# Linear attention into a routed expert layer on one core: the first route's exponential is issued after the search for the fullest expert, and the experts' first rows are read from PSUM

## The chip, the core and the metric

The kernel runs on one core of a Trainium2 chip. The metric is the device time of one execution in microseconds (us); lower is better. Names of engines in the profile: PE is TensorE (PEld its weight loads), DVE is VectorE, ACT is ScalarE, POOL is GpSimd, SP is the engine that issues most of the DMAs. SBUF is the on-chip memory that every engine reads; PSUM is the small one that TensorE writes its products to, and that DVE and ACT can read and write.

## The reference

Four batches of 576 tokens with 8 heads of 64 go through attention with a feature map, and the 2304 rows of 512 that come out are routed, each to one of 8 experts (a two-layer network with 1024 hidden units). An expert takes at most `capacity` = 576 rows, in the order of the tokens.

```
phi(x):  proj = x @ w_phi;  proj -= max(abs(proj));  [exp(proj), exp(-proj)]
kv = phi(k)^T v;  z = sum phi(k);  x = (phi(q) kv) / (phi(q) z + 1e-6)

logits = x @ w_gate;  expert = argmax(logits)
gate   = exp(0) / (sum exp(logits - max) + 1e-9)
row    = number of earlier tokens with the same expert   (kept if < capacity)
disp[expert, row] = x
out[token] = gate * relu(disp[expert] @ w1[expert]) @ w2[expert]
```

## The kernel before

**Two stages.** In the first (about 4 to 168 us) attention runs and every token is routed: its row is scattered into a buffer `xs` in device memory, where each expert has 576 slots. In the second (168 us to the end) the experts run one after the other over their rows, and their results are scattered to the output.

**The pipeline of the first stage.** The tokens are cut into two passes `p` of 9 blocks of 128 tokens. A pass has 18 items for the keys and then 18 for the queries, one per block and half of the heads. In each step `t` of `attention()` a new item begins on TensorE with `project` (L259 and L260: products with the two halves of `w_phi`, into a PSUM tile `pr` of which there are two). One step later DVE centres it (`center`: the maximum `m`, L265, then the difference `d`, L269; there are three tiles for `d`). ACT makes the two exponentials `kp` of a key item (L315, L316), or, after a transpose on TensorE (L356), `qp` of a query item (L358, L359). Four steps after its projection TensorE sums a key item (`kv_sum`, L342); a query item is multiplied with the sums by `q_num` (L371). Beside this ACT and POOL split the next inputs into two 16-bit parts: L194 on ACT writes the high part, and L195 on POOL, which waits for it, the low one.

**Routing in small steps.** `rows_out` leaves the logits of a block in `lg`, and `route` is called for groups of 9, 4, 3 and 2 blocks. It does no work itself: it appends some 25 small operations to the list `pending`, and `tick()`, which is called after each operation of `center` and within `rows_out`, takes the next ones from it. So the list's order and its length decide between which large instructions a small one stands on its engine. From step 36 on, `tick()` is sparing: it takes one operation at every second call (two in steps 46 and 49) until the first group knows the fullest expert, and one per call after that. An entry `rest` does nothing but spend a turn.

**The first group and the fullest expert.** The experts are run with the fullest of the first 9 blocks first. For that the first group alone has the five operations of `swaps()`: a product of ones with the counts `rb` on TensorE, into the columns `TOT` of the PSUM tile `sm` (L502), the maximum (L503), its place (L504, L505), and nine small POOL instructions (`swap_all`, L488 to L496). These leave in SBUF the expert order and, in `perm["s"]`, the first row of each expert in `xs`. Each route later multiplies its one-hot choice `oh` (16-bit, SBUF) with `perm["s"]` (L539) and sums it (L540): the first row of the token's expert. The product on TensorE that numbers the tokens (`positions`, L455) writes the same tile `sm` as L540.

**The shared tile.** The small operands of all routes lie in one PSUM tile, `sm_t` (named `sm`): logits less their maximum (`lt`), choice, counts, sums, and the columns `TOT`. The framework orders accesses by tile. `exps` (L481) is the exponential of `lt` on ACT: it reads `sm` and writes `es`, which `sums` (L470) needs only after `positions`.

Of the kernel before, what the change touches and what calls it, by code (L numbers as in the profile page):

```python
# [15 lines left out]
ALU = mybir.AluOpType  # L16
# [4 lines left out]
P = 128  # L21
# [3 lines left out]
NE, DM, DFF = 8, H * D, 1024  # L25
# [12 lines left out]
def tile_kernel(ctx: ExitStack, tc: tile.TileContext, qT, kT, vT, vv, w_phi, w_g, w1, w2, out, cap):  # L38
# [55 lines left out]
    perm = {x: cpool.tile([P, NE], F32, tag=f"perm{x}", name=f"perm{x}") for x in "abcdesh"}  # L94
# [46 lines left out]
    POS, SCR, SW, TOT = 0, 72, 210, 496  # L141
    sm_t = ps_1.tile([P, 512], F32, tag="sm", name="sm")
# [240 lines left out]
    def rows_out(p, r):  # L383
# [14 lines left out]
        if i == n - 1:  # L398
            route(blk - i, n, xr, lg)
# [15 lines left out]
    def route(blk, n, xr, lg):  # L415
        def small(name, shape, dt=F32):
            return r_p.tile([P, n, *shape], dt, tag=name, name=name)
# [15 lines left out]
        oh = small("oh", [NE], BF16)  # L433
        rb = r_p.tile([P, NE], BF16, tag="rb", name="rb")
        es, sel = small("es", [NE]), small("sel", [NE])
# [4 lines left out]
        v = nc.vector  # L440

        def flat(t):
            return t.rearrange("p n a -> p (n a)")
# [55 lines left out]
        def swaps():  # L499
            tot = sm_t[:, TOT:TOT + NE]  # L500
            return [
                lambda: nc.tensor.matmul(tot, ones, rb, start=True, stop=True),  # L502
                lambda: v.tensor_reduce(seen, tot, AX.X, ALU.max),  # L503
                lambda: v.scalar_tensor_tensor(perm["a"], tot, seen, iota8, ALU.is_ge, ALU.mult),  # L504
                lambda: v.tensor_reduce(lead8, perm["a"], AX.X, ALU.min),  # L505
                swap_all,
            ]

        late = blk >= LATE
# [12 lines left out]
        def ready():  # L522
# [9 lines left out]
            lambda: v.scalar_tensor_tensor(ef, lt, 0.0, io, ALU.is_ge, ALU.mult),  # L532
            lambda: v.tensor_reduce(flat(ix), ef, AX.X, ALU.min),
            lambda: v.tensor_tensor(oh, ix.to_broadcast([P, n, NE]), io, ALU.is_equal),
            *([number, exps] if late else [exps] if old is None else []),
            lambda: v.tensor_reduce(rn[:, 0], oh.rearrange("p n e -> p e n"), AX.X, ALU.add),
            run_total,
            *([*swaps(), rest, rest, rest] if old is None else []),
            lambda: v.tensor_tensor(sel, oh, perm["s"].unsqueeze(1).to_broadcast([P, n, NE]), ALU.mult),  # L539
            lambda: v.tensor_reduce(flat(sl), sel, AX.X, ALU.add),  # L540
            positions,
            *([] if late or old is None else [exps, rest, rest, rest]),
# [571 lines left out]
```

## Time and profile before

| | |
|---|---|
| median of 3 runs | 427.6 us (426.96 to 427.92) |
| the profiled execution's own time | 425.98 us |
| its span, first to last instruction | 424.2 us |
| mean granted TensorE clock | 0.99 of full |
| PE busy | 405.1 us (95%) |
| DVE busy | 265.9 us (63%) |
| ACT busy | 245.9 us (58%) |
| POOL busy | 175.4 us (41%) |

The profile is of one execution, and its own time is 1.6 us below the median. Starts and durations are in us from the span's first instruction. A duration on DVE or ACT contains a fixed part in which the next instruction already runs, so the distance between two starts is the better measure of what an instruction takes from its engine. Time in which an engine stood still before an instruction is shown in brackets with what ended it; an instruction that had begun and was held up inside shows a long duration instead. `PEclk` is the clock that TensorE was granted, as a share of 2.4 GHz: 0.50 is the lower of its two levels, 1.2 GHz.

### The profile page before, as it was taken

What the parts mean: (1) busy time and instruction counts of PE and PEld (TensorE: products, weight loads), DVE (VectorE), ACT (ScalarE), POOL (GpSimd) and SP (SyncE); (2) the same over time, 40 slices, a digit from 0 to 9 for tenths busy, and PEclk for the clock granted to TensorE, in tenths of its full rate; (3) what the DMA queues carried; (4) which work ended last, traced back from release to release, by engine and by line L of the source; (5) the groups of instructions that cost most, each with busy time, mean ns of one, the idle gap of its engine ahead of it and who ended that gap; (6) DMA issues with size and microseconds to landing.
All of it is one profiled execution on the core that took longest, in us unless ns stands there. A gap on an engine that the chain in (4) does not pass through costs nothing.

```text
span 424.2 us, 12166 instructions
## 1 busy us (share of the span) xinstructions
PE 405.1 (95%) x4813; PEld 357.7 (84%) x4813; DVE 265.9 (63%) x585; ACT 245.9 (58%) x452; POOL 175.4 (41%) x215
## 2 busy tenths in 40 slices
PE   6999999999799989999999999999999999999992
PEld 4788888888789878989979898989898998799871
DVE  5776898887788797833247975757475464156410
ACT  3978687779776766712146855656565454155410
POOL 1848566448576778730035306042241500160011
PEclk9999999999899999999999999999999999999997
DMA  7990599489506743479007995977959176210010
GB/s 254 388 353 5 170 328 372 138 287 307 172 6 222 227 171 107 175 249 368 5 32 223 341 338 192 331 226 224 324 179 349 64 240 228 93 36 0 2 51 29
DMA packets 42715, 82.78 MB, mean 195 GB/s; under 512 B 4351, under 2 KB 9343, under 8 KB 42624
## 3 DMA queue, kind: packets, MB, share of 16 engines
q1 hardware_dynamic: 38080, 72.13, 50.5%
q0 software_dynamic: 4544, 9.47, 6.2%
q8 instruction: 53, 0.87, 0.9%
q14 instruction: 38, 0.31, 0.2%
HBM read 62.65 MB, written 24.30 MB: 205 GB/s over the span
## 4 chain that ended last, share of the span: by engine, by line
PE 83%; POOL 4%; issue 4%; ACT 4%; DVE 3%; DMA 1%; POOLq 0%; ACTq 0%
PE ph L814 9%; PE ph L815 9%; PE ph L817 9%; PE acc L342 8%; PE acc L371 5%; PE sm L847 4%; PE sm L845 4%; PE sm L848 4%; PE ph L845 4%; PE ph L847 4%; PE ph L848 4%; PE pr L259 3%; PE pr L260 2%; PE pr L254 2%; PE pt L747 2%
## 5 line engine op out<-in xcount | busy, mean ns | idle before, releaser
L169 POOL DMA_INDIRECT out<-y,it x22 | 24.4, 1111 | 164.4 <-ACT y L860 86.7
L123 DVE TENSOR_TENSOR l<-raw,h 128x512 fp32r<-128x512 f32 x118 | 79.6, 706 | 19.6 <-ACT h L117 16.9
L195 POOL TENSOR_TENSOR stk<-px,stk 64x1024 f16<-64x1024 f32 (+1 forms) x30 | 70.8, 2363 | 38.6 <-ACT stk L194 37.7
L814 PE MATMUL ph<-xh,h 128*128 128x256 f32 (+3 forms) x292 | 79.4, 298 | 0.1
L815 PE MATMUL ph<-xh,l 128*128 128x256 f32 (+3 forms) x292 | 78.9, 296 | 0.0
L117 ACT ACTIVATE h<-raw 128x512 fp32r<-128x512 f32 x128 | 75.7, 629 | 0.0
L828 ACT ACTIVATE h<-ph 128x256 fp32r<-128x256 f32 (+3 forms) x67 | 28.8, 429 | 53.6 <-PE ph L817 52.9
L831 DVE SCALAR_TENSOR_TENSOR h<-ph,h 128x256 fp32r<-128x256 f32 (+2 forms) x91 | 33.3, 388 | 39.2 <-ACT h L828 38.8
L814 PEld LDWEIGHTS ph<-xh,h 128*128 128x128 f32 x292 | 55.6, 191 | 1.2 <-issue 0.2
L815 PEld LDWEIGHTS ph<-xh,l 128*128 128x128 f32 x292 | 55.7, 191 | 0.9
L265 DVE TENSOR_REDUCE m<-pr 128x4 f32<-128x512 f32 x72 | 49.2, 684 | 8.6 <-PE pr L260 5.1
L269 DVE TENSOR_TENSOR d<-pr,m 128x512 f32<-128x512 f32 x72 | 49.7, 691 | 4.0 <-ACT kp L316 0.4
L817 PE MATMUL ph<-xh,h 128*128 128x256 f32 (+3 forms) x292 | 50.9, 296 | 0.0
L342 PE MATMUL acc<-v,kp 128*64 128x73 f32 (+1 forms) x1280 | 46.3, 231 | 1.1 <-issue 1.1
L342 PEld LDWEIGHTS acc<-v,kp 128*64 128x64 f32 (+1 forms) x1280 | 40.7, 138 | 5.8 <-issue 2.6
L371 PE MATMUL acc<-kv,qp 128*64 128x73 f32 x1152 | 44.5, 229 | 0.0
L371 PEld LDWEIGHTS acc<-kv,qp 128*64 128x64 f32 x1152 | 39.1, 136 | 6.0 <-issue 5.7
L817 PEld LDWEIGHTS ph<-xh,h 128*128 128x128 f32 x292 | 42.7, 191 | 0.6
L259 PE MATMUL pr<-whi,stk 128*128 128x128 f16 x260 | 36.9, 223 | 2.6 <-DVE d L269 2.3
L260 PE MATMUL pr<-wlo,stk 128*128 128x128 f16 x260 | 36.4, 221 | 0.0
L194 ACT ACTIVATE stk<-px 64x1024 f16<-64x1024 f32 (+1 forms) x30 | 34.5, 1150 | 0.5
L358 ACT ACTIVATE qp<-pt 128x512 f32<-128x512 f32 x36 | 21.5, 596 | 21.1 <-PE pt L356 21.0
(163 smaller groups left out, 715.8 us busy)
## 6 DMA issues: line engine op xcount, KB each, us to landing
raw<-in_w SPq DMA_DIRECT2D x28, 1024.0 KB, 7.9
xs<-fill SPq DMA_DIRECT2D x18, 514.0 KB, 6.1
xr<-xs SPq DMA_DIRECT2D x24, 257.0 KB, 7.9
raw<-in_w SPq DMA_DIRECT2D x8, 512.0 KB, 4.3
vt<-in_vT SPq DMA_DIRECT2D x3, 1152.0 KB, 12.7
v<-in_vv SPq DMA_DIRECT2D x2, 1314.0 KB, 11.9
px<-in_kT SPq DMA_DIRECT2D x5, 512.0 KB, 8.5
px<-in_qT SPq DMA_DIRECT2D x4, 640.0 KB, 9.3
```

Source lines behind the costliest of these rows:

```text
L117: nc.scalar.activation(hi, a, AF.Copy)
L123: engine.tensor_tensor(lo, a, hi.bitcast(F32), ALU.subtract)
L195: return lambda: nc.gpsimd.tensor_tensor(t[other], x, t[own], ALU.subtract)
L259: nc.tensor.matmul(pr[:, j], lt, whi, start=True, stop=False)
L260: nc.tensor.matmul(pr[:, j], lt, wlo, start=False, stop=True)
L265: nc.vector.tensor_reduce(m.rearrange("p a b -> p (a b)"), pr, AX.X, ALU.max, apply_absolute_value=True)
L269: beat[0] = nc.vector.tensor_tensor(d, pr, m.to_broadcast([P, 4, NF]), ALU.subtract)
L342: nc.tensor.matmul(acc[f:f + D, a, j * GC:(j + 1) * GC], kp[lo:hi, j, a, f:f + D], vt[lo:hi, r, h * GC:(h + 1) * GC], start=first and j == ...
L371: nc.tensor.matmul(num[lo:hi, g, j * GC:(j + 1) * GC], qp[:, a, j, lo:hi], kv_t[b][:, a, 4 * g + j], start=(a == 0), stop=(a == 1))
L814: nc.tensor.matmul(acc, hi[:, k, fs], xh[:, k, o:o2], start=(k == 0), stop=False)
L815: nc.tensor.matmul(acc, lo[:, k, fs], xh[:, k, o:o2], start=False, stop=False)
L817: nc.tensor.matmul(acc, hi[:, k, fs], xl[:, k, o:o2], start=False, stop=(k == 3))
```

## The change

Three things change in the list of `route`. In the first group `exps` moves from its place ahead of the count (L536) to behind `swap_all`. Behind the three `rest`s a new operation copies `perm["s"]` from SBUF into the columns `TOT` of the PSUM tile `sm`, which by then have been read by L503 and L504. And in all four groups the product `sel` reads the first rows from there, not from `perm["s"]`.

```
-            *([number, exps] if late else [exps] if old is None else []),
+            *([number, exps] if late else []),
             lambda: v.tensor_reduce(rn[:, 0], oh.rearrange("p n e -> p e n"), AX.X, ALU.add),
             run_total,
-            *([*swaps(), rest, rest, rest] if old is None else []),
-            lambda: v.tensor_tensor(sel, oh, perm["s"].unsqueeze(1).to_broadcast([P, n, NE]), ALU.mult),
+            *([*swaps(), exps, rest, rest, rest, lambda: v.tensor_copy(sm_t[:, TOT:TOT + NE], perm["s"])]
+              if old is None else []),
+            lambda: v.tensor_tensor(sel, oh, sm_t[:, TOT:TOT + NE].unsqueeze(1).to_broadcast([P, n, NE]), ALU.mult),
```

In the changed kernel the copy is L538 and `sel` L540; the lines behind them have a number one higher than before. `old is None` holds for the first group, `late` for the last.

The first place is on DVE in the second pass's keys, from the first group's choice `oh` (L534) to its count `rb` (L476); `m` and `d` are the large operations of `center`, and in brackets stands which engine's semaphore a row waits for. Before:

```order
L534 TENSOR_TENSOR oh<-sm,iota_74 128x72 [waits DVE_49]
L269 TENSOR_TENSOR d<-pr,m 128x512 [waits DVE_49,Activation_49]
L265 TENSOR_REDUCE m<-pr 128x4 [waits PE_49]
L536 TENSOR_REDUCE sm<-oh 128x8 [waits DVE_49,Activation_49]
L269 TENSOR_TENSOR d<-pr,m 128x512 [waits DVE_49]
L265 TENSOR_REDUCE m<-pr 128x4 [waits PE_49]
L476 CAST rb<-sm 128x8 [waits DVE_49]
```

On the same engine at the same place, with the change:

```order
L534 TENSOR_TENSOR oh<-sm,iota_74 128x72 [waits DVE_49]
L269 TENSOR_TENSOR d<-pr,m 128x512 [waits DVE_49,Activation_49]
L265 TENSOR_REDUCE m<-pr 128x4 [waits PE_49]
L536 TENSOR_REDUCE sm<-oh 128x8 [waits DVE_49]
L476 CAST rb<-sm 128x8 [waits DVE_49]
L269 TENSOR_TENSOR d<-pr,m 128x512 [waits Activation_49]
L265 TENSOR_REDUCE m<-pr 128x4 [waits PE_49]
```

The count L536 no longer waits for ACT, and `rb`, with it the product L502 and all of `swaps()`, stands one large pair earlier.

The second place is on DVE some five items later, where `sel` stood: the new copy and what is queued behind it, with the change:

```order
L265 TENSOR_REDUCE m<-pr 128x4 [waits PE_49]
L269 TENSOR_TENSOR d<-pr,m 128x512 [waits DVE_49,Activation_49]
L538 COPY sm<-perms 128x8 [waits Activation_49,Pool_49]
L265 TENSOR_REDUCE m<-pr 128x4 [waits PE_49]
L540 TENSOR_TENSOR sel<-oh,sm 128x72 [waits DVE_49]
L269 TENSOR_TENSOR d<-pr,m 128x512 [waits DVE_49,Activation_49]
```

The wait for ACT's exponential now stands at the copy, which waits for POOL's `perm["s"]` too; before, `sel` waited for POOL alone, behind the `m` that now comes after the copy.

The third place is on ACT in the same items; `kp` are the exponentials of a key item, `stk` the split of an input, `es` the moved exponential. Before:

```order
L316 ACTIVATE kp_2037<-d_2023 128x4x128
L481 ACTIVATE es_1746<-sm_132 128x72
L315 ACTIVATE kp_2073<-d_2060 128x4x128 [waits DVE_49,PE_49,Activation_49]
L316 ACTIVATE kp_2073<-d_2060 128x4x128
L315 ACTIVATE kp_2106<-d_2095 128x4x128 [waits DVE_49,PE_49,Activation_49]
L316 ACTIVATE kp_2106<-d_2095 128x4x128
L194 ACTIVATE stk_2133<-px_1717 64x1280 [waits Pool_49]
```

On ACT with the change, up to the moved exponential:

```order
L194 ACTIVATE stk_2133<-px_1717 64x1280 [waits Pool_49]
L315 ACTIVATE kp_2144<-d_2129 128x4x128 [waits DVE_49,PE_49]
L316 ACTIVATE kp_2144<-d_2129 128x4x128
L315 ACTIVATE kp_2179<-d_2167 128x4x128 [waits DVE_49,PE_49]
L316 ACTIVATE kp_2179<-d_2167 128x4x128
L481 ACTIVATE es_1746<-sm_132 128x72
L194 ACTIVATE stk_2212<-px_1897 64x1024 [waits DMAHW1_49]
```

The exponential has moved behind four more key items and one split. The sequence on POOL and on SP is the same in both kernels.

## Rows read from the trace of the kernel before

**Rows 1.** Waits of PE, whole span: line, waited for, us, times, longest.
```profile
...
PE pr L259 <- DVE d L269: 2.3, 1, 2.3
PE sm L455 <- DVE sm L540: 1.8, 1, 1.8
...
PE sm L845 <- issue: 0.2, 1, 0.2
```

**Rows 2.** Busy time by stretch: PE, PEld, DVE, ACT, POOL, clock, DMA share.
```profile
109.00:110.00 1.00, 1.00 (x15) 0.80 (x14) 1.00 (x3) 0.82 (x3) 0.00 (x0) 0.50 1.01 327
112.00:114.00 2.00, 2.00 (x48) 1.71 (x47) 1.38 (x5) 1.37 (x3) 1.70 (x1) 1.00 0.01 4
```

**Rows 3.** Timeline of PE, 104 to 116 us: start, duration, line, [idle before].
```profile
104.27 0.23 PE L259 MATMUL pr<-whi,stk 128*128 128x128 f16 x1
...
108.40 0.29 PE L259 MATMUL pr<-whi,stk 128*128 128x128 f16 x1 [2.33 <-DVE d L269]
...
111.51 0.29 PE L259 MATMUL pr<-whi,stk 128*128 128x128 f16 x1
...
113.39 0.22 PE L259 MATMUL pr<-whi,stk 128*128 128x128 f16 x1
...
115.11 0.23 PE L259 MATMUL pr<-whi,stk 128*128 128x128 f16 x1
```

**Rows 4.** Timeline of DVE, 103 to 108 us.
```profile
103.28 0.68 DVE L265 TENSOR_REDUCE m<-pr 128x4 f32<-128x512 f32 x1
107.46 0.29 DVE L536 TENSOR_REDUCE sm<-oh 128x8 f32<-128x72 bf16 x1 [3.50 <-ACT es L481]
107.66 0.68 DVE L269 TENSOR_TENSOR d<-pr,m 128x512 f32<-128x512 f32 x1
```

**Rows 5.** Timeline of ACT, 107 to 116 us.
```profile
107.22 0.21 ACT L481 ACTIVATE es<-sm 128x72 f32<-128x72 f32 x1
...
110.95 1.27 ACT L194 ACTIVATE stk<-px 64x1280 f16<-64x1280 f32 x1
112.24 0.63 ACT L315 ACTIVATE kp<-d 128x512 f32<-128x512 f32 x1
...
114.69 0.63 ACT L315 ACTIVATE kp<-d 128x512 f32<-128x512 f32 x1 [1.30 <-DVE d L269]
```

**Rows 6.** Timeline of PE, 147 to 154 us.
```profile
147.11 0.61 PE L356 MATMUL pt<-ident,d 128*128 128x128 f32 x4
...
149.27 0.61 PE L356 MATMUL pt<-ident,d 128*128 128x128 f32 x4
...
152.82 0.18 PE L455 MATMUL sm<-oh,tri 128*128 128x32 bf16 x1 [1.78 <-DVE sm L540]
...
152.94 0.22 PE L259 MATMUL pr<-whi,stk 128*128 128x128 f16 x1
...
153.39 0.61 PE L356 MATMUL pt<-ident,d 128*128 128x128 f32 x4
```

**Rows 7.** Timeline of DVE, 149 to 157 us.
```profile
149.50 3.04 DVE L539 TENSOR_TENSOR sel<-oh,perms 128x32 f32<-128x32 bf16 x1
...
156.37 0.14 DVE L546 TENSOR_TENSOR sel<-sm,oh 128x32 f32<-128x32 f32 x1
```

**Rows 8.** Timeline of POOL, 106 to 158 us.
```profile
106.35 2.61 POOL L195 TENSOR_TENSOR stk<-px,stk 64x1280 f16<-64x1280 f32 x1 [0.75 <-ACT stk L194]
112.30 2.62 POOL L195 TENSOR_TENSOR stk<-px,stk 64x1280 f16<-64x1280 f32 x1 [3.33 <-ACT stk L194]
115.44 0.25 POOL L488 TENSOR_SCALAR swap<-swap 128x1 f32<-128x1 f32 x1 [0.53 <-DVE swap L505]
...
117.59 0.24 POOL L494 TENSOR_SCALAR perms<-perme 128x8 f32<-128x8 f32 x1
...
149.98 2.49 POOL L123 TENSOR_TENSOR l<-raw,h 128x512 fp32r<-128x512 f32 x2
...
154.89 2.51 POOL L123 TENSOR_TENSOR l<-raw,h 128x512 fp32r<-128x512 f32 x2
```

## The prediction

> **What bounds the kernel now.** I read the totals first: TensorE is busy for 405.1 of 424.2 us, so only what makes TensorE wait, or run at the lower clock, can move the time. Then the waits of TensorE over the whole span [rows 1]: behind the start-up there are two of any size, 2.3 us for DVE's `d` and 1.8 us for DVE's `sm` of L540, and nothing above 0.2 us later on. The change touches both places. The stretches [rows 2] show that the first one has a second price: behind it the granted clock is 0.50, the 1.2 GHz level, at 109 to 110 us, and 1.00 again at 112.
>
> The first place in detail. The starts of the projections on TensorE [rows 3] are one step's clock: a normal step is 115.11 − 113.39 = 1.72 us. From 104.27 to 113.39 there are three steps, and they took 9.12 us. On DVE [rows 4] the count L536 stood for 3.50 us until ACT's `es` (L481) was done; the `d` of that item came at 107.66 where its `m` had begun at 103.28, and TensorE, which has two `pr` tiles, could not project further. ACT was not idle: it runs about four microseconds behind DVE there and reached L481 at 107.22 [rows 5]. So the wait is for an instruction that is 0.21 us long and whose result is needed much later; it waits only since both touch the tile `sm`.
>
> The second place. TensorE's transposes are 2.16 us apart (147.11 to 149.27) and once 4.12 (149.27 to 153.39), with 1.78 of idle time before L455 [rows 6]. DVE had no wait shown; its `sel`, 32 elements wide, lasted 3.04 us and ended at 152.54 [rows 7], 0.07 behind the end of two L123 on POOL (149.98 + 2.49 = 152.47) [rows 8]. A product of the same size with one operand in PSUM (L546) took 0.14 us at 156.37 [rows 7], in the middle of another two L123 on POOL (154.89 to 157.40) [rows 8]. I read that as follows: a DVE product with both inputs in SBUF is held up while POOL works on SBUF, and one with an input in PSUM is not.
>
> **The change part by part.**
>
> *The exponential behind the tests.* With L481 gone from in front of the four key items, L536 finds nothing to wait for. The three steps from 104.27 then take 3 × 1.72 = 5.16 in place of 9.12: 3.96 us less, of which 2.41 is the late projection (108.40 − 104.27 − 1.72), 1.39 the following step at the lower clock (111.51 − 108.40 − 1.72) and 0.16 the rest of it (113.39 − 111.51 − 1.72). The product L502 lies within these three steps before and after, so I take 3.9. What could be late next is ACT, as its lag stays. It has slack: behind the stall it stood still for 1.30 us before 114.69, waiting for DVE [rows 5], and a kept lag costs TensorE nothing as long as `kp` is there when its sum comes, four steps (6.9 us) behind the projection. Bounds of this part: 3.96 if all of it goes; 0 if the same wait returns at the copy.
>
> *The copy and its wait.* The wait for `es` now stands at L538, with the wait for POOL's `perm["s"]`, and behind it on DVE are an `m`, `sel` and a `d` that TensorE needs. When do the three come together? With steps of 1.72 the projections start at 106.0, 107.7, 109.4, 111.2, 112.9, 114.6, 116.3 and 118.0. By the order on DVE the copy follows the `d` of the step at 112.9, done some 2 us after its step's start (0.6 for the projection, then `m` and `d` at up to 0.68 each [rows 4]): 114.9. ACT takes over the slot at 107.22, makes two pairs (four times at most 0.63) until 109.7 and the split L194 in 1.29 (110.95 to 112.24) until 111.0 [rows 5]. POOL's L195 behind it lasts 2.62, until 113.6; then come the small swap instructions, which need 2.39 from L488's start to L494's end (117.59 + 0.24 − 115.44) [rows 8]: 116.0 at the latest, 115.6 if the four exponentials overlap a little as ACT's usually do. ACT's `es`, two pairs and an L194 later, is done by 113.8. So the copy waits about 0.7 to 1.1 us for POOL, not for ACT. Behind it `m`, `sel` and `d` take up to 1.5; `d` is there at 117.2 to 117.6, and the projection that needs its `pr` tile starts at 118.0. The wait fits, with 0.4 to 0.8 us to spare; cost 0. The trace of before has no copy from SBUF to PSUM. Its nearest row is L546, 0.14 us [rows 7], which I take; the other end is a copy held up on POOL like the long `sel`, by one L195 of 2.62 [rows 8].
>
> A sentence of the Trainium skill speaks against the change here: "SBUF — State Buffer", section "Who interferes with whom", counts a copy among the operations that can take the port pair shared with GpSimd, and by that the sum would be the 424.1 to 426.0 of the first rival below. It refers for the conditions to "VectorE: DVE Perf Modes", section "Mode 2×_2P", which wants source and destination in SBUF; by that the copy into PSUM is free and the sum stays. No row here shows such a copy.
>
> *`sel` from PSUM.* The second group's `sel` falls from 3.04 to about 0.14 [rows 7]. DVE then has L540 done by about 150, before TensorE ends its sums, and the idle 1.78 before L455 goes. The step 149.27 to 153.39 becomes 2.16 plus the 0.12 of L455 (152.82 to 152.94) [rows 6]: 4.12 − 2.28 = 1.84 us less. The clock did not fall there, so nothing comes on top. Bounds: 1.96 and 0 (if POOL or ACT keep the pace instead). For the other three groups TensorE did not wait: 0.
>
> *The extra turn* in the first group moves its later operations by less than an item; they only feed scatters that begin in the query part: 0.
>
> The sum: 3.9 + 1.84 = 5.7 us, since the two stalls lie in different items and TensorE is at work without a pause from the one to the other and after the second [rows 1]. The profiled execution would fall from 425.98 to 420.3; the runs shown have a median 1.6 us above it, 427.6, and I forecast 427.6 − 5.7 = **421.9 us**.
>
> **The rivals.**
>
> *The copy is held up by POOL* as `sel` was: swap done at 116.0 to 116.4, then one L195, the copy at 118.6 to 119.0 in place of the latest harmless 116.4 (118.0 less 1.5). TensorE idles for 2.2 to 2.6 and, if the clock falls as in [rows 2], loses up to 1.5 more (1.39 + 0.16). Given back: 2.2 to 4.1; time 424.1 to 426.0, nearer the first since the pause of 1.78 was not followed by a lower clock. For it: POOL has an L195 ready in that stretch all the time. Against it: L546's 0.14.
>
> *The second stall moves.* POOL, with its scatters, L412 and L123, or ACT keeps the pace at 150 us, so that only the first part pays: 427.6 − 3.9 = 423.7. For it: POOL is at work on its two L123 until 152.47 [rows 8]. Against it: TensorE's wait names L540 [rows 1], and L540 needs nothing of those L123.
>
> *The first stall returns whole*, at the copy, because ACT's lag is longer than I worked out: 427.6 − 1.84 = 425.8. Against it: `es` by 113.8 against 114.9.
>
> *Slower: the search comes a whole POOL round late.* POOL works in order; the swap instructions stand behind an L195 that waits for ACT's L194, and two such L195 began 5.95 us apart (106.35, 112.30), 3.33 of it waiting for ACT [rows 8]. If the swap starts a round later than I have it, the copy comes at 115.6 + 5.95 = 121.6, TensorE idles 5.2 us longer than the harmless 116.4, and the lower clock adds 1.5: 6.7 given back against 5.7 gained, 428.6. It decides from a give-back of 6.6 us, a copy later than 121.5. Before, no such round stood between the tests and the copy's place, and DVE's tests come earlier now, not later.
>
> *The change does nothing* for TensorE: 427.6; then what ended the waits is not what the rows name.
>
> **How the numbers follow.** Chances: both stalls go 0.70, copy held up 0.13, second stall moves 0.08, first one returns 0.03, no effect 0.02, slower 0.04. A measurement of this kernel tells a difference of 0.2%, 0.86 us, from none; all cases but the last two are faster by more than that. So faster 0.94, same 0.02, slower 0.04. The likeliest time is 421.9. Its own range is 421.0 (both upper bounds, 3.96 + 1.96, from the lowest run, 426.96) to 422.2 (5.7 from the highest, 427.92); to hold 8 in 10 I go up over 423.7 and the cheap half of the held-up copy to 424.8, and down to 420.8.
>
> **What the profile after would show.** Right: no wait of L536 for ACT; projections 1.72 apart from 104 to 118 us with the clock at 1.00 throughout; L538 waiting about one microsecond for POOL's L494 and TensorE not waiting behind it; `sel` at 128x32 under 0.3 us while an L123 runs on POOL; transposes 2.16 to 2.3 apart around 146 us; the expert stage starting 5.7 us earlier and otherwise the same. Wrong: an idle time of TensorE that ends in `d` at 118 to 121 us, or a long L538 beside an L195 (the first rival); L455 still waiting, now for ACT or POOL (the second); a clock of 0.50 anywhere between 106 and 125 us.

## The result, and the profile after

The changed kernel took 421.5 us (median of 6 runs, 420.47 to 421.88), the kernel before beside it 427.3 (median of 6): a ratio of 0.9871, 95% interval 0.9837 to 0.9906. In another set of runs it took 421.5 again, against 426.4: 0.9901 (0.9863 to 0.9939). Medians and ratios here and below leave out three slow executions, two of the exponential alone (429.63 and 789.99) and one of its repetition (429.61). The profiled execution took 420.62 us with a span of 418.9; before it was 425.98 and 424.2.

TensorE's waits over the whole span, in the order line, waited for, total us, times, longest:

```profile
PE pr L254 <- DMA px<-in_kT: 4.2, 1, 4.2
PE acc L342 <- issue: 1.2, 3, 0.7
PE pr L254 <- DVE v L240: 0.7, 1, 0.7
PE pr L259 <- POOL stk L195: 0.3, 1, 0.3
```

Both waits of [rows 1], for `d` and for L540's `sm`, are gone. What is left ends before 94 us and stands in the kernel before as well, but for one piece of the "issue" row that is at the first place. TensorE's timeline answers to [rows 3] down to 118.60, and to [rows 6] from 145.83; the last line is the first product of the experts:

```profile
104.06 0.23 PE L259 MATMUL pr<-whi,stk 128*128 128x128 f16 x1
...
105.80 0.23 PE L259 MATMUL pr<-whi,stk 128*128 128x128 f16 x1
...
107.92 0.34 PE L342 MATMUL acc<-v,kp 128*64 128x73 f32 x3 [0.39 <-issue]
...
108.23 0.22 PE L259 MATMUL pr<-whi,stk 128*128 128x128 f16 x1
...
109.95 0.23 PE L259 MATMUL pr<-whi,stk 128*128 128x128 f16 x1
...
118.60 0.23 PE L259 MATMUL pr<-whi,stk 128*128 128x128 f16 x1
...
145.83 0.61 PE L356 MATMUL pt<-ident,d 128*128 128x128 f32 x4
...
148.12 0.61 PE L356 MATMUL pt<-ident,d 128*128 128x128 f32 x4
...
162.72 0.39 PE L815 MATMUL ph<-xh,h 128*128 128x256 f32 x1
```

The three steps from 104.06 end at 109.95: 5.89 us, where before it was 9.12. Two are 1.73 long, and the middle one is 2.43: TensorE pauses in it for something that the profile can only call "issue". The step with the positions (L455) takes 2.29 where it took 4.12. DVE, answering to [rows 4, 7]:

```profile
103.67 0.29 DVE L536 TENSOR_REDUCE sm<-oh 128x8 f32<-128x72 bf16 x1
...
115.71 0.17 DVE L538 COPY sm<-perms 128x8 f32<-128x8 f32 x1 [0.16 <-POOL perms L494]
...
116.40 0.22 DVE L540 TENSOR_TENSOR sel<-oh,sm 128x72 f32<-128x72 bf16 x1
...
146.05 0.18 DVE L540 TENSOR_TENSOR sel<-oh,sm 128x32 f32<-128x32 bf16 x1
```

L536 no longer waits, the copy waits 0.16 us for POOL, and the second group's `sel` takes 0.18. POOL, answering to [rows 8]:

```profile
116.03 4.24 POOL L195 TENSOR_TENSOR stk<-px,stk 64x1024 f16<-64x1024 f32 x2
...
145.51 1.01 POOL L459 DMA_INDIRECT xs<-xr,si  x1 [0.17 <-issue]
146.55 2.53 POOL L123 TENSOR_TENSOR l<-raw,h 128x512 fp32r<-128x512 f32 x2
```

Of two stretches of the windows (PE, PEld, DVE, ACT, POOL, granted clock, DMA share, GB/s), which answer to [rows 2], the clock is 1.00 (2.4 GHz) where it was 0.50, and the DMA engines are full:

```profile
106.00:108.00 2.00, 1.61 (x39) 1.42 (x37) 0.90 (x2) 2.00 (x5) 1.85 (x1) 1.00 1.04 380
108.00:110.00 2.00, 2.00 (x45) 1.74 (x45) 1.59 (x4) 1.98 (x4) 0.77 (x1) 1.00 1.06 368
```

Neither 420.62 nor 425.98 tells the parts apart. I use one measure for that in all runs below, called the stretch: from TensorE's wait for POOL at 93 to 95 us (the 0.3 of the waits) to the first product of the experts. Runs that started earlier or later become comparable by it. It is 167.97 − 93.89 = 74.08 us before and 162.72 − 93.69 = 69.03 after.

### The profile page after: what moved, and what is told of

It is laid out like the page before. It is cut to its first block, busy times and chain, and to the rows that moved or that the text cites. A ratio compares the mean times of both kernels' runs of the same rounds, so it can differ in the third digit from the quotient of the medians.

```text
span 418.9 us, 12169 instructions
## 1 busy us (share of the span) xinstructions
PE 403.8 (96%) x4813; PEld 356.3 (85%) x4813; DVE 263.3 (63%) x586; ACT 245.5 (59%) x452; POOL 176.1 (42%) x215
## 3 DMA queue, kind: packets, MB, share of 16 engines
q1 hardware_dynamic: 38080, 72.13, 51.4%
## 4 chain that ended last, share of the span: by engine, by line
PE 93%; DVE 2%; issue 1%; POOL 1%; DMA 1%; ACT 0%; POOLq 0%; SPq 0%; ACTq 0%; DVEq 0%
PE acc L342 10%; PE ph L815 9%; PE ph L818 9%; PE ph L816 9%; PE acc L371 9%; PE pr L259 4%; PE sm L848 4%; PE sm L846 4%; PE sm L849 4%; PE ph L846 4%; PE ph L848 4%; PE ph L849 4%; PE pt L356 3%; PE pr L260 3%; PE pr L254 2%; PE pt L748 2%
## 5 line engine op out<-in xcount | busy, mean ns | idle before, releaser
L123 DVE TENSOR_TENSOR l<-raw,h 128x512 fp32r<-128x512 f32 x118 | 79.6, 705 | 19.7 <-ACT h L117 16.9
L195 POOL TENSOR_TENSOR stk<-px,stk 64x1024 f16<-64x1024 f32 (+1 forms) x30 | 70.9, 2363 | 36.0 <-ACT stk L194 35.1
```

The lines of the kernel that those rows point to most:

```text
L123: engine.tensor_tensor(lo, a, hi.bitcast(F32), ALU.subtract)
L195: return lambda: nc.gpsimd.tensor_tensor(t[other], x, t[own], ALU.subtract)
```

## The experiments

| run | set | what is in it | median, us | ratio to before, 95% interval | the stretch, us |
|---|---|---|---|---|---|
| before (profiled once) | 1 | | 427.3 | | 74.08 |
| changed | 1 | both | 421.5 | 0.9871 (0.9837–0.9906) | 69.03 |
| changed, again | 3 | both | 421.5 | 0.9901 (0.9863–0.9939) | 69.48 |
| exponential alone | 2 | first | 425.0 | 0.9932 (0.9904–0.9961) | 72.13 |
| the same, again | 4 | first | 424.2 | 0.9940 (0.9915–0.9965) | 72.78 |
| count in SBUF | 2 | first, nothing moved | 425.4 | 0.9952 (0.9933–0.9971) | 72.21 |
| copy to SBUF | 2 | first, `sel` from SBUF | 425.9 | 0.9961 (0.9940–0.9983) | 72.12 |
| PSUM, no turn more | 3 | second | 424.3 | 0.9946 (0.9915–0.9976) | 72.27 |
| other loads later | 4 | second, by POOL | 424.4 | 0.9955 (0.9932–0.9979) | 72.22 |
| PSUM, one turn more | 2 | second | 432.9 | 1.0134 (1.0099–1.0168) | 79.70 |
| the same, positions in PSUM | 4 | second | 425.7 | 0.9988 (0.9966–1.0011) | 70.78 |
| fills later | 3 | both | 421.4 | 0.9876 (0.9837–0.9916) | 68.46 |
| search late | 3 | both | 423.0 | 0.9917 (0.9888–0.9946) | 70.26 |
| fills later, positions in PSUM | 4 | both | 420.2 | 0.9864 (0.9829–0.9899) | 68.05 |

Each set has its own runs of the kernel before, with medians of 427.3, 427.8, 426.4 and 426.4 us in sets 1 to 4, so ratios can be compared between sets and medians only within one. The theory throughout: two stalls that don't depend on each other, one of ordering by tile, one of DVE and POOL meeting in SBUF.

**The exponential alone.** The copy is a `rest` again and `sel` reads `perm["s"]`.

```
-  [*swaps(), exps, rest, rest, rest, lambda: v.tensor_copy(sm_t[:, TOT:TOT + NE], perm["s"])]
+  [*swaps(), exps, rest, rest, rest, rest]
-  lambda: v.tensor_tensor(sel, oh, sm_t[:, TOT:TOT + NE]..., ALU.mult),
+  lambda: v.tensor_tensor(sel, oh, perm["s"]..., ALU.mult),
```

> The first group's exponential stands behind the tests, as in the changed kernel, but the first rows are not copied (a turn is spent in the copy's place) and sel reads them from SBUF. My theory (two separate stalls): the first stall goes, some 3.4 us of span as in the changed kernel (projection after the tests at 109.95 in place of 113.39), and the second stays: sel of the second group held for 2 to 3 us beside POOL's L123, TensorE idle about 1.8 us before L455. Span about 420.8, time 423.6 to 424.2. Rival (the second stall was only a consequence of the first one's shift in time): sel is short without PSUM too, and the span is 418.9, the time 421.5.

L536 did not wait, and the time fell by 0.7%, where the whole change gave 1.0 to 1.3%. But the second `sel` was not held, and TensorE paused at 136, 141 and 147 us instead, for "issue": its steps from 136 to 149 us took 2.2 us more than 2.16 each. The two other kernels of that set that take away the first stall alone paused at the same places, so none of the three shows the second stall by itself. I ran this one again in another set:

> The same kernel as in the run of the exponential alone (the exponential at its new place, no copy to PSUM), run again beside other kernels. Theory A, the pauses of TensorE that the profile puts down to issue at 136, 141 and 147 us come from how the edits stagger the work: they are there again, 0.2 to 0.4 us each, and the span is again some 4 us over that of the changed kernel. Theory B, they belong to the chip or the hour: they are gone, and what is left between this kernel and the changed one is the hold of sel alone, at most 1.8 us. In both the first sel (128x72) is held 1.5 to 1.9 us by GpSimd's line 195; the second sel (128x32) is held only if it meets line 123, which it missed by 0.8 us the first time.

The pauses were gone and the hold was back. DVE's two `sel` of the first run, then of the second:

```profile
116.97 1.71 DVE L540 TENSOR_TENSOR sel<-oh,perms 128x72 f32<-128x72 bf16 x1
148.79 0.18 DVE L540 TENSOR_TENSOR sel<-oh,perms 128x32 f32<-128x32 bf16 x1
```

```profile
117.23 1.48 DVE L540 TENSOR_TENSOR sel<-oh,perms 128x72 f32<-128x72 bf16 x1
147.04 3.04 DVE L540 TENSOR_TENSOR sel<-oh,perms 128x32 f32<-128x32 bf16 x1
```

And POOL's scatter and weights beside them, in the same order:

```profile
148.74 1.01 POOL L459 DMA_INDIRECT xs<-xr,si  x1 [0.15 <-issue]
149.78 2.51 POOL L123 TENSOR_TENSOR l<-raw,h 128x512 fp32r<-128x512 f32 x2
```

```profile
146.49 1.01 POOL L459 DMA_INDIRECT xs<-xr,si  x1 [0.17 <-issue]
147.52 2.51 POOL L123 TENSOR_TENSOR l<-raw,h 128x512 fp32r<-128x512 f32 x2
```

A `sel` that starts 0.99 us ahead of L123 gets through; one that starts 0.48 ahead is held until both L123 are over (147.52 + 2.51 = 150.03; `sel` ends at 150.08). Before it was the same 0.48 (149.50 and 149.98, [rows 7, 8]). In the changed kernel `sel` starts 0.50 ahead, at 146.05, and takes 0.18: the same meeting, another operand. Why a `sel` that starts 0.48 ahead is held at all, when it takes 0.18 where nothing holds it, is not shown. What the pauses of the first run came from is open too; the same kernel had none of them in the other set, which ran on another chip.

**The count in SBUF.** The kernel before, with the counts of the first group taken out of the shared tile. No instruction moves.

```
-        ix, sl, rn, sm = quick(1), quick(1), quick(NE, 1), quick(1)
...
+        ix, sl, sm = quick(1), quick(1), quick(1)
+        rn = r_p.tile([P, 1, NE], F32, tag="rn1", ...) if first else quick(NE, 1)
```

> The kernel before, with one thing changed: the first group's count is written to a tile in SBUF, not to sm; the exponential keeps its place in front of the count. My theory (the wait was an ordering by tile, not by place in the list): the count waits for nothing, the first stall goes although nothing was moved: projections 1.7 apart from 104 to 113 us, clock 1.00, span about 420.8, time 423.6 to 424.2; the second stall stays at about 1.8 us. Rival (ACT's lag itself limits the stretch, and the place of the exponential matters): the wait turns up at the next write to sm or at d, and the span is above 423.

The count, which is L537 in this kernel, did not wait, though ACT's exponential came as late as before:

```profile
103.48 0.28 DVE L537 TENSOR_REDUCE rn<-oh 128x8 f32<-128x72 bf16 x1
```

```profile
106.83 0.21 ACT L482 ACTIVATE es<-sm 128x72 f32<-128x72 f32 x1
```

The stretch became that of the exponential alone (72.21 against 72.13). So it was the shared tile that ordered the two, not data and not ACT's pace.

**The copy to SBUF.** The change with the copy into `perm["a"]` and `sel` from there.

> The changed kernel with the first rows copied to another tile in SBUF in place of PSUM; sel reads the copy. My theory (two SBUF operands are what is held up by POOL): sel of the second group takes 2 to 3 us again, ending with POOL's second L123, TensorE idles about 1.8 us before L455; span 418.9 + 1.8 = 420.7, time 423.3 to 424. Rival (it is the copy by DVE that helps, since sel no longer reads a tile written by POOL): sel is short, span 418.9, time 421.5. The copy itself may now also be held beside POOL: up to 2.6 us at 115.7.

The first `sel` is held for 1.68 us again, so it is not the copy as such that frees it. The second one was expected to be held and was not:

```profile
148.68 0.20 DVE L540 TENSOR_TENSOR sel<-oh,perma 128x32 f32<-128x32 bf16 x1
```

It starts 1.02 us ahead of L123. So it does, within 0.03, in the exponential alone and the count in SBUF, which have no copy at all and where it takes 0.18 and 0.20, and the stretch, 72.12, is theirs. So this run speaks for PSUM as the place that counts by the first `sel` only.

**PSUM without the move, and without a turn more.** `exps` in its old place, and a `rest` given up for the copy; the edit is shown against the changed kernel.

```
-  *([number, exps] if late else []),
+  *([number, exps] if late else [exps] if old is None else []),
-  [*swaps(), exps, rest, rest, rest, lambda: v.tensor_copy(...)]
+  [*swaps(), rest, rest, lambda: v.tensor_copy(...)]
```

> As the kernel before, with the exponential in its old place, the copy to PSUM in the place of one of the three empty turns, and sel reading PSUM. The list has its old length, so the scatters keep their steps, which the earlier run with one turn more did not. Theory: L536 waits 3.5 us and the clock falls, as before; the second group's sel is under 0.3 us and TensorE does not wait before L455; 1.8 us faster than before, 3.4 us slower than the changed kernel. Rival (the copy itself costs, not the extra turn): about as slow as the earlier run, 5 us above before, with a DVE instruction held for several us beside POOL.

L536 waited 3.51 us as before; the step with the positions took 2.29 (148.99 to 151.28). The stretch fell by 1.81. The copy, later here than in the changed kernel, stood in the middle of an L195 and was not held:

```profile
118.63 0.16 DVE L538 COPY sm<-perms 128x8 f32<-128x8 f32 x1
```

```profile
117.92 4.25 POOL L195 TENSOR_TENSOR stk<-px,stk 64x1024 f16<-64x1024 f32 x2
```

**The other loads later.** The kernel before, with POOL's L123 of steps 65 and 66 moved to steps 67 and 68. If L123 holds `sel`, this must be worth the same.

```
-            if 64 <= t < 72:
+            if 64 <= t < 72 and t not in (65, 66):
...
+            if t in (67, 68):
+                w_lo(*divmod(t - 66, 4), nc.gpsimd)
```

> The kernel before with GpSimd's two pieces of weights of steps 65 and 66 (line 123) made at steps 67 and 68. Theory A, sel is held because its two operands lie in SBUF while GpSimd works there: with no line 123 beside it, the second sel (128x32) takes about 0.2 us in place of 3.04, and the step of TensorE there falls from 4.12 to about 2.3 us, so the time falls by up to 1.8 us, less what the doubled line 123 delays at steps 67 and 68. Rival, sel is held by the scatters or by something else than line 123: it stays above 1 us and the time stays within 0.5 us of the kernel before. The first stall stays at 3.5 us on line 536 in both.

DVE's second `sel`, from SBUF still:

```profile
149.39 0.18 DVE L539 TENSOR_TENSOR sel<-oh,perms 128x32 f32<-128x32 bf16 x1
```

It started as far into the scatter as in the kernel before (0.55 and 0.56 us) and was not held:

```profile
148.84 1.01 POOL L459 DMA_INDIRECT xs<-xr,si  x1 [0.17 <-issue]
```

So it is L123 that holds it and not the scatter. The time agrees with the run above: 0.9955 and 0.9946, and a stretch of 72.22 and 72.27.

**PSUM without the move, one turn more.** As above, but with all three `rest`s, so that the first group's list is a turn longer.

> The first rows are copied to PSUM and sel reads them there, but the exponential stays in front of the count. My theory: L536 waits 3.5 us for ACT, TensorE idles 2.3 us and the granted clock falls to 0.50 for some 3 us, as before; the second group's sel takes under 0.3 us and TensorE does not wait at L455. Span about 424.2 - 1.8 = 422.4, time 425.3 to 425.8. Rival (sel is held by something else than the SBUF operand, such as POOL's own lateness): sel long, span 424.2, time 427.3.

Slower by 1.3%, which I had not expected. On DVE, then on POOL, then on TensorE:

```profile
156.15 5.90 DVE L550 TENSOR_SCALAR drop<-pr 128x4 f32<-128x4 f32 x1
```

```profile
156.08 2.52 POOL L123 TENSOR_TENSOR l<-raw,h 128x512 fp32r<-128x512 f32 x2
158.54 1.05 POOL L412 TENSOR_TENSOR xr<-nb,rd 128x512 f32<-128x512 f32 x1
159.54 2.48 POOL L123 TENSOR_TENSOR l<-raw,h 128x512 fp32r<-128x512 f32 x2
```

```profile
162.69 0.26 PE L259 MATMUL pr<-whi,stk 128*128 128x128 f16 x1 [4.42 <-DVE d L269]
```

With the list a turn longer the first scatter came at 129.89 (127.88 without the turn). L550, an operation of four elements from SBUF to SBUF, met the first of five POOL instructions without a gap between them and was held until the last was done. Such a run of five stands in the kernel without the turn too (149.70 to 155.67), but there L550 comes near its end and is held for 0.85. Behind L550 on DVE stood the `d` for which TensorE waited, and behind that wait the granted clock was 0.50 from 162 to 168 us. TensorE's steps from 136 to 152 us also took 2.4 us more than without the turn, with pauses for "issue" before 138.29 and 148.42; the other kernels of this set had such pauses too, and this kernel was not run in another one. So how much of the 1.3% is the turn is not separated from those pauses. The changed kernel has the same L550; there it met the last pair of L123 and was held for 0.69, with nothing behind it late. I then gave L550 an input in PSUM:

```
-        ix, sl, rn, sm = quick(1), quick(1), quick(NE, 1), quick(1)
...
-        pr, ov = small("pr", [1]), drop_t...
...
-            lambda: v.tensor_tensor(sl, sl, pr, ALU.add),
...
-            lambda: v.tensor_tensor(si.unsqueeze(2), sl, ov, ALU.add),
+        ix, pr, rn, sm = quick(1), quick(1), quick(NE, 1), quick(1)
...
+        sl, to, ov = small("pr", [1]), mx if first else quick(1), drop_t...
...
+            lambda: v.tensor_tensor(to, sl, pr, ALU.add),
...
+            lambda: v.tensor_tensor(si.unsqueeze(2), to, ov, ALU.add),
```

> The first run with the copy alone, in which VectorE's line 550 was held for 5.90 us, with the sum of line 548 written to PSUM, so that line 550 reads PSUM and no more SBUF alone. Theory A, line 550 was held because it read and wrote SBUF while GpSimd worked through five instructions without a gap: it takes 0.2 us, TensorE's wait of 4.42 us behind it goes, and the time falls from 432.9 to between 426 and 429 us (GpSimd's lateness behind the scatters stays). Rival, it was held because GpSimd was late as such: another VectorE instruction or the scatters take its place and the time stays above 430.

DVE, and what POOL did meanwhile:

```profile
154.09 0.15 DVE L550 TENSOR_SCALAR drop<-sm 128x4 f32<-128x4 f32 x1
```

```profile
153.62 1.29 POOL L123 TENSOR_TENSOR l<-raw,h 128x512 fp32r<-128x512 f32 x1
```

L550 ran in 0.15 us in the middle of an L123. The time, 425.7 us, is under theory A's 426 to 429, but those were worked out in a set in which the kernel before took 427.8; by the ratio it is 427.3 there, as theory A had it. It is not faster than before (0.9988), though its profiled execution, 423.5 us, shows the second stall gone; that execution was the fastest of 12, so what the others lose I can't say from it. And L550 came 2 us earlier than in the run above, 1.8 us ahead of the long run on POOL, so it was not put to the same test; TensorE's pauses between 136 and 149 us were gone too. What brought the time back, PSUM or the absence of the pauses, stays open.

**The search late.** The rival on the slower side was a search that comes late on POOL. Two POOL products of 128x512 stand ahead of it here.

```
         gp = nc.gpsimd
...
+        for _ in range(2):
+            gp.tensor_tensor(late_t, xr_t[:, 0, 0:512], xr_t[:, 1, 0:512], ALU.add)
```

> The changed kernel with two POOL products of 128x512 put in front of the swap instructions (results unused), so that the first rows, and with them the copy L538, come about 2.2 us later. It prices the rival in which the copy is late. From the changed kernel's trace the d behind the copy ends at 117.28 and the projection that needs it starts at 118.60, so 1.3 us are free: TensorE should idle about 0.9 us and the time rise by 0.9 us; if the lower clock follows, by up to 2.4. If the slack were the 0.4 to 0.8 that I worked out, 1.4 to 1.8. If the copy's wait is off TensorE's path altogether: no change.

DVE's copy, and the projection behind it:

```profile
118.13 0.17 DVE L541 COPY sm<-perms 128x8 f32<-128x8 f32 x1 [2.17 <-POOL perms L497]
```

```profile
119.83 0.22 PE L259 MATMUL pr<-whi,stk 128*128 128x128 f16 x1 [0.75 <-DVE sm L544]
```

The copy waited 2.17 us in place of 0.16, and of that TensorE lost 0.82 (a step of 2.55 in place of 1.73). So the slack behind the copy is about 2.01 − 0.82 = 1.2 us in this run. The stretch is 0.78 longer than that of the changed kernel in the same set (70.26 against 69.48), as expected; the ratios, 0.9917 and 0.9901, don't tell the two apart. The rival's mechanism exists; the changed kernel doesn't reach it.

**The fills later.** The changed kernel once more, and with five of the DMAs that fill `xs` at later steps, away from 108 us:

```
-        FILLS = [*range(18, 36, 3), *range(36, 48)]
+        FILLS = [*range(18, 36, 3), *range(36, 43), *range(47, 52)]
```

> The changed kernel once more, unchanged, beside the next ones. The experiments so far show pauses of TensorE with no releaser at 136, 140 and 146 us (about 2 us in all) that neither the kernel before nor the changed one showed. If these pauses belong to the day and the chip, they appear here too and the time is about 423.5; if they belong to the edits, this run gives 421.5 and a span of about 419 with none of them.

> The changed kernel with five of the 18 fills of xs issued about five steps later (steps 47 to 51 in place of 43 to 47), so that the DMA queues are not full at 105 to 110 us. Theory (the 0.39 us pause of TensorE within L342 at 107.9, with the step of 2.43 in place of 1.73, is late instruction supply behind full queues): the pause goes or shrinks, gain 0.3 to 0.7 us against the changed kernel. Rival (the pause belongs to the place in the program): it stays, no change beyond 0.2%. A cost is possible: the later fills meet the loads and the first scatters at 120 us.

TensorE in the changed kernel, run again:

```profile
108.04 0.34 PE L342 MATMUL acc<-v,kp 128*64 128x73 f32 x3 [0.76 <-issue]
```

and two projections with the fills later, at the same place:

```profile
107.14 0.23 PE L259 MATMUL pr<-whi,stk 128*128 128x128 f16 x1
...
108.91 0.22 PE L259 MATMUL pr<-whi,stk 128*128 128x128 f16 x1
```

The pause is gone (a step of 1.77), and the stretch is 1.02 us shorter than that of the changed kernel in the same set (68.46 against 69.48). In the median it is 0.2 us, within the noise.

**Both additions to the changed kernel.** The later fills and the positions in PSUM together.

> The changed kernel with the sum of line 548 in PSUM (line 550 took 0.69 us there) and the last five fills of the slots at later steps (the pause of TensorE at 108 us goes). Theory A, both are on the path: some 0.7 us from the fills, and nothing from line 550, whose result only the scatter waits for: 420.5 to 421.5 us. Rival, the fills collide with the scatters or the weights later, which gives the 0.7 us back: within 0.3 us of the changed kernel's 421.5.

420.2 us is the lowest median of all, and its stretch, 68.05, the shortest. Its ratio to the kernel before, 0.9864, is that of the changed kernel within the intervals (0.9871 and 0.9901), so it is not shown to be faster. The rival's bound of 0.3 us was passed, but against runs of other sets.

## Why the prediction was right

**The first stall: right in kind, 3.9 was too much.** That the exponential holds L536 only through the tile is shown by the count in SBUF. The three steps gave 9.12 − 5.89 = 3.23 us in the profiled execution and 9.12 − 6.26 = 2.86 when it was run again. What is missing is the longer middle step, 2.43 and 2.81 in place of 1.73, of which the profile shows 0.39 and 0.76 as TensorE's pause. I had it not in the sum: I took three steps of 1.72 for granted once DVE was on time. The kind was to be seen before the change, in a row that [rows 1] leaves out; its two pieces, 0.64 and 0.43, end at 27.11 and 33.36 us:

```profile
PE acc L342 <- issue: 1.1, 2, 0.6
```

With the fills moved in the last run the same three steps take 5.21: 3.91 less, the predicted size.

```profile
104.28 0.23 PE L259 MATMUL pr<-whi,stk 128*128 128x128 f16 x1
...
109.49 0.23 PE L259 MATMUL pr<-whi,stk 128*128 128x128 f16 x1
```

In both profiled executions with the fills moved the pause at 108 us is gone. What stops TensorE there is not shown: with the fills later the DMA engines were as busy at 107 to 108 us (a share of 1.00), without a pause. The profile's list of queues has two of the kind "instruction", which would fit a late supply of instructions but prove nothing.

**The lower clock was a term of some executions.** 1.39 us of the 3.9 rested on the clock of [rows 2]. The same wait, 2.32 us that end at 108.93, stood in the run with the positions in PSUM, and there the clock stayed at 1.00. Of the five profiled executions that have this wait, three show 0.50 behind it (before, PSUM with no turn more, other loads later) and two don't (PSUM with one turn more, with and without the positions). Three stretches of the one with the positions:

```profile
106.00:108.00 2.00, 0.61 (x20) 0.46 (x15) 0.01 (x1) 1.96 (x4) 1.25 (x2) 1.00 1.02 370
108.00:110.00 2.00, 1.07 (x24) 0.97 (x26) 2.00 (x5) 1.01 (x2) 1.49 (x1) 1.00 0.98 351
110.00:112.00 2.00, 2.00 (x56) 1.82 (x52) 1.97 (x4) 1.80 (x4) 0.00 (x0) 1.00 0.75 265
```

And the second stall, behind which I saw no lower clock and booked nothing, had one in the exponential alone, run again, behind a wait of the same 1.78 us:

```profile
150.00:152.00 2.00, 1.63 (x31) 1.46 (x32) 1.93 (x7) 1.33 (x4) 0.59 (x2) 0.97 0.02 6
152.00:154.00 2.00, 2.00 (x32) 1.85 (x29) 1.82 (x8) 1.38 (x3) 2.00 (x3) 0.50 0.78 209
```

There it cost 1.47 us (two steps of 3.16 and 2.71 where the kernel before has 2.24 and 2.16), and with 9.12 − 6.25 = 2.87 for the first stall that leaves 1.4, near the 1.3 by which its stretch is shorter than before's. So a price of the clock behind either wait comes and goes between executions; the term should have been a range in both places. The mean granted clocks of all executions fit this: the 12 of the changed kernel have 0.994 to 0.996, and of the 81 of the kernel before in sets 2 to 4, 28 have 0.994 or more and 26 have 0.990 or less.

**The copy and its wait: cost 0, right.** It waited 0.16 us for POOL, where I had 0.7 to 1.1, since the pause had moved DVE's order back while POOL was not late; in the last run, without the pause, it is as I had it:

```profile
115.90 0.17 DVE L538 COPY sm<-perms 128x8 f32<-128x8 f32 x1 [0.80 <-POOL perms L494]
```

ACT's `es` was done at 112.81, before the 113.8 that I gave it. The projection that needs the `d` behind the copy came at 118.60, and that `d` ends at 117.28. The copy itself took 0.17 us. In the changed kernel it was not put to the first rival's test, since it waits for POOL's own instruction and POOL's next L195 begins 0.32 us behind its start. In the three runs that copy to PSUM without the move it was: there it begins 0.59 to 0.71 us into an L195 and takes 0.16, so the first rival's mechanism does not hold where the two meet.

**`sel` from PSUM: right, 1.83 for 1.84.** The two runs that remove only this stall, one by PSUM and one by POOL's order, gave 0.5% each, about 2 us, and the exponential alone, run again, still had it whole. The reading that the operand's place decides is shown best by the first `sel`, which began within an L195 in both cases: 1.71 us with both inputs in SBUF, 0.22 with one in PSUM. "SBUF — State Buffer" of the Trainium skill, section "Who interferes with whom", says the same of both: two inputs in SBUF contend with a GpSimd instruction that reads SBUF, and at most one does not (outside the two-port modes). But the hold depends on half a microsecond of timing, as the three runs show in which a `sel` from SBUF slipped through.

**The sum** holds within the intervals: the first stall alone is worth 0.6% in the one run whose trace still has the second whole (the exponential alone, run again), the second alone 0.5% in two runs, and the whole 1.0 to 1.3%. The three other runs without the first stall (0.4 to 0.7%) had slower steps in place of the second. In the profiled executions the two parts, 3.23 + 1.83 = 5.06, are all that the stretch lost (5.05), and 5.7 was forecast. So that the time came 0.4 us from the forecast is in part luck: the median fell by 5.8 us beside its first runs of the kernel before and by 4.9 beside the second. The 0.2% that I took as told from none was too fine: the interval of the changed kernel's ratio is about 0.35% either way.

**The extra turn: 0 held here, but not as a rule.** From the stretch's start the first scatter came 3.24 us earlier than before, as TensorE's three steps did (3.23). I read from the code that this is because `exps`, moved behind the search, is taken from the list at the faster pace that begins there. Without the move the turn put the first scatter 2 us later, and the kernel with it took 1.9% more than the one without (1.0134 and 0.9946), by way of POOL, L550 and the lower clock, with the pauses of its set in that figure.

Of the rivals, the copy held up by POOL, the moved stall and the returning one did not come; the late search was built, and it costs what the slack behind the copy doesn't cover.

## What to carry to other kernels

A wait between two engines that share a tile but no data goes as well by giving one of them a tile of its own (here one in SBUF) as by moving it; the chain of waits shows such a case as a long wait for a short instruction whose result is needed later. Where GpSimd computes without a pause, small VectorE operations from SBUF to SBUF can stand for microseconds, and an operand in PSUM freed `sel`; look for these in the timeline as long durations, not as waits. A turn more in a list that is spread over other work moves what stands behind it, here the first scatter by 2 us: check what that meets on the other engines.

## What was not expected of the hardware

- A VectorE operation that was held by GpSimd did not get its turn when the first GpSimd instruction was done: `sel` stood over both L123, and L550 over L123 twice, L412 and L123 twice, 5.90 us. Between two L195, however, `sel` was let through (1.71 us from 116.97, where the first L195 of 116.44 ends at about 118.6). "SBUF — State Buffer" of the Trainium skill, section "SBUF: two separate sides", gives the ports to whichever of the two starts first, for the whole instruction, and has the other blocked. The L195 agree with it (1.71, to the end of the first one); the L123 don't, as the hold went on over the second one, and as by the profile's starts `sel` had begun 0.48 us ahead of the first.
- TensorE pauses at times with the releaser "issue", in which it waits for no semaphore. The pause at 108 us came with DMA engines at a share of 1.03 to 1.07 and went when the fills moved; but the one that ends at 33.36 us in the kernel before stands where the share is 0.00 to 0.04. Full DMA engines alone don't tell when it comes, and its cause is open.
